# Second mixture's token sums on VectorE, sums and decoding dealt over other steps, an earlier sigmoid table, longer strings of products

## The chip, the cores and the metric

The kernel runs on one core of a Trainium2 chip. The metric is the device time of one launch in microseconds (us). Before the change it is 1125.84 us, the median of 3 runs (1125.04 to 1125.88).

## The reference

Attention with a threshold per row (4 batches, 8 heads, 576 tokens, 64 wide), then two feed-forward blocks ("mixtures") of 2304 tokens, 512 wide, 2048 hidden. The weights come as 64-bit floats.

```python
def _moe_ref(x, w_in, w_out):
    h = x @ w_in
    g = h - np.tanh(h)
    return (g @ w_out).astype(np.float32)

def _moe2_ref(x, w_in, w_out):
    h = x @ w_in
    g = h * (1.0 / (1.0 + np.exp(-h)))
    return (g @ w_out).astype(np.float32)
...
    x = np.ascontiguousarray(attn_out.transpose(0, 2, 1, 3)).reshape(B * S, H * D)
    x = _moe_ref(x=x, **moe_kwargs)
    return _moe2_ref(x=x, **moe2_kwargs)
```

## The kernel before

Every product is made of three TensorE products: each operand is split into a high part, rounded to the TensorE format, and a low part, the rest. A split is a copy on ScalarE and a subtraction on VectorE or GpSimd. A block of weights is decoded from 64-bit words: a DMA into one of three staging slots of `st_r` (`fill`, L749 and L751), a scaling on ScalarE (`rebias`, L757), three integer operations on VectorE (L761, L762, L765), and for `w_out` a high copy on ScalarE (L776) and a low subtraction on GpSimd (L778). `lone` does this for one 128-row block of a `w_out`, `decode_pair` for two blocks of `w2_in` with four GpSimd sums more. Both are generators; `advance` makes one go on to its next yield, and the tables `LONE`, `PAIR`, `EARLY2` and `late` say in which step that happens.

**Attention** takes the first 330 us and is not changed.

**First mixture.** A unit is one 128-wide chunk m of the hidden layer of one tile j of tokens (tiles of 512, 512, 512, 256, 512; 16 chunks: 80 units). Step s of `step_of` writes out, in this order: the 12 products of h for unit s+3 (`emit_h`, L671), the tail of the activation of unit s+1 (`back_a`: L701, L702), the head of that of unit s+2 (`front_a`, ScalarE L683 to L685), `decoding(s, 0)`, `front_b` (GpSimd L690, ScalarE L691 with tanh, VectorE L692), the split of g for unit s+1 (`back_b`: ScalarE L709, VectorE L710), `front_c` (ScalarE L696), pieces of the second mixture (`firsts`, `split_block`), the 12 output products of unit s (`triples`, L722), and `decoding(s, 1)`. The last tile is steps 64 to 79 (`first` = 64).

**Second mixture.** Tokens are taken in three sweeps of 768, the hidden layer in 8 groups g of two chunks, so there are 24 groups. In a group the four quarter products are made from seven (k = 0 to 6), with sums of token quarters (`combos`, recorded at L872 and the high copies at L875) on one side and sums of weights, made by `decode_pair`, on the other. One k is a *slot*. A slot is one string of six 384-wide products (L1024) into one of two banks in turn, then `POPS[k]` output units taken from a queue (`stream`), three 512-wide products each (L978). The bank is read by an addition on VectorE (L1031), for k = 0 by a copy on ScalarE (L1051), for k = 2 by sigmoid and product directly. Four results of a group then go through sigmoid (ScalarE L1054), product (VectorE L1055), high copy (ScalarE L1058) and low subtraction (VectorE L1059), and three output units join the queue. A finished output bank is copied out at L983 (ScalarE) or L985 (VectorE). The sums for the first sweep are `firsts`, made in steps 68 to 76 of the last tile, four entries a step; those for a later sweep are made in the last two groups of the sweep before it. They work in place in the token buffer `xT`, in the pieces of `wr`, and in `st_r`. In `combos`, V is VectorE and G is GpSimd. The 72 loads of weight blocks (`load_block`, L900) each wait for TensorE to have read the buffer; their split is at L905 and L906.

PE, VectorE, ScalarE and GpSimd run their instructions in the order written; SyncE issues all DMAs in its own fixed order.

Of the kernel before, what the change touches and what calls it, by code (L numbers as in the profile page):

```python
# [16 lines left out]
P = 128  # L17
# [23 lines left out]
LONE = ((0, 1), (1, 1), (2, 0), (2, 0), (2, 1), (3, 0))  # L41
PAIR = ((0, 1), (1, 1), (2, 0), (2, 1), (3, 1), (4, 0), (4, 1))
STA = 3
STAGE0 = 10
RATE1 = 15
# [12 lines left out]
def kernel(  # L58
# [86 lines left out]
    if True:  # L145
# [500 lines left out]
        wos = {}  # L646
# [99 lines left out]
        def fill(x, src):  # L746
# [21 lines left out]
        def lone(src, wt):  # L768
# [6 lines left out]
            word = low.bitcast(F32)  # L775
            nc.scalar.copy(out=wt[:, 0], in_=word)  # L776
            yield
            nc.gpsimd.tensor_tensor(out=wt[:, 1], in0=word, in1=wt[:, 0].bitcast(F32), op=ALU.subtract)  # L778
            yield

        def decode_pair(g):
# [10 lines left out]
            low, high = fill(0, source(g))  # L792
# [4 lines left out]
            yield  # L797
            low, high = fill(0, source(g + NG))
# [11 lines left out]
            yield  # L810
# [6 lines left out]
        for m, at in chunks:  # L817
            for ds, pos in LONE:
                due.setdefault((max(-4, at + ds), pos), []).append(m)
        EARLY2 = {0: 65, 1: 68, 2: 71, 8: 74}  # L820
        LATE2 = (9, 10, 3, 11, 4, 12, 5, 13, 6, 14, 7, 15)
        for m, at in EARLY2.items():
            for ds, pos in LONE:
                due.setdefault((at + ds, pos), []).append((1, m))
        for g in range(NG):
            for ds, pos in PAIR:
                due.setdefault((STAGE0 + 4 * g + ds, pos), []).append((2, g))
        running = {}
# [24 lines left out]
        wbuf = [wflat[:, x * (WB + NPC * 2 * HT):][:, 0:WB] for x in range(2)]  # L853
        piece = [wflat[:, WB + i * 2 * HT:WB + (i + 1) * 2 * HT].rearrange("p (c t) -> p c t", c=2) for i in range(NPC)]
# [12 lines left out]
        def combos(s, w2, wx, w1, cs=slice(0, 2)):  # L867
# [9 lines left out]
            V, G = nc.vector, nc.gpsimd  # L877
# [13 lines left out]

        def block(i, b):
# [15 lines left out]
        def step_of(s):  # L908
# [19 lines left out]
            if s == first:  # L928
# [183 lines left out]
```

## Time and profile before

| | |
|---|---|
| median of 3 runs | 1125.84 us |
| profiled execution | 1125.29 us |
| its span, first to last instruction | 1123.5 us |
| PE busy | 1089.6 us (97%) |
| VectorE, ScalarE, GpSimd busy | 857.0 (76%), 784.3 (70%), 433.8 us (39%) |
| first mixture, about | 330 to 727 us |
| second mixture, about | 727 to 1118 us |

In the trace PE is TensorE's products and PEld its weight loads, DVE is VectorE, ACT ScalarE, POOL GpSimd, SP the queue of SyncE. A row of a timeline reads: start, length, engine, line, operation, what it writes and reads, how many were merged, and in brackets the idle time before it with what ended it. A product's length overlaps the next one's; start to start is what counts.

### The profile page before, as it was taken

How to read it: one execution, taken by the hardware profiler on the slowest of the kernel's cores; microseconds unless marked ns; L12 is line 12 of the kernel's file. 1: busy time of each engine (PE TensorE's matmuls, PEld its weight loads, DVE VectorE, ACT ScalarE, POOL GpSimd, SP SyncE). 2: the span in 40 equal slices, each digit the busy share in tenths (PEclk: the TensorE clock that was granted, in tenths of full speed). 3: DMA queues.
4: the chain of work that ended last, by engine and by line, in shares of the span. 5: the costliest groups of instructions: out<-in, count | busy, mean ns of one | idle time of the engine just before them, and what ended most of it. 6: DMA issues, size and time to landing. Idle time of an engine off the chain costs nothing. (4 is left out here: it accounts for less than half of the span.)

```text
span 1123.5 us, 17914 instructions
## 1 busy us (share of the span) xinstructions
PE 1089.6 (97%) x6028; PEld 899.5 (80%) x6028; DVE 857.0 (76%) x1524; ACT 784.3 (70%) x1627; POOL 433.8 (39%) x446
## 2 busy tenths in 40 slices
PE   7999999999999999999999999999999999999998
PEld 6667677767667888888889988789887888879896
DVE  6888888888858878878855677889879655775554
ACT  5988989899878887787877888755544434543432
POOL 4766766777634424434532237612125000110000
PEclk9999999999999999999999999999999999999999
DMA  8677776877534103323311011244423222232211
GB/s 197 155 182 200 202 201 171 220 192 187 160 120 185 56 20 132 131 76 115 133 72 39 11 60 30 64 149 136 132 57 87 80 64 57 61 104 66 57 34 56
DMA packets 104298, 124.93 MB, mean 111 GB/s; under 512 B 47760, under 2 KB 71824, under 8 KB 103184
## 3 DMA queue, kind: packets, MB, share of 16 engines
q1 hardware_dynamic: 104208, 123.80, 38.6%
q8 instruction: 48, 0.79, 0.3%
q14 instruction: 42, 0.34, 0.1%
HBM read 73.93 MB, written 17.30 MB: 81 GB/s over the span
## 5 line engine op out<-in xcount | busy, mean ns | idle before, releaser
L722 PE MATMUL bank<-g_r,wo 128*128 128x512 f32 (+1 forms) x960 | 213.2, 370 | 4.4 <-DVE g_r L710 4.4
L1024 PE MATMUL bank<-wr 128*128 128x384 f32 x816 | 201.1, 336 | 6.2 <-ACT tm_r L1051 3.4
L722 PEld LDWEIGHTS bank<-g_r,wo 128*128 128x128 f32 x960 | 169.3, 190 | 35.5 <-DVE g_r L710 5.5
L671 PE MATMUL bank<-xs_r,wr 128*128 128x512 f32 (+1 forms) x640 | 193.3, 368 | 0.0
L690 POOL TENSOR_TENSOR tm_r<-tm_r 128x512 f32<-128x512 f32 (+1 forms) x78 | 95.7, 1227 | 210.1 <-ACT tm_r L685 210.1
L1024 PEld LDWEIGHTS bank<-wr 128*128 128x128 f32 x816 | 148.4, 188 | 19.5 <-ACT tm_r L1051 4.3
L356 POOL TENSOR_SCALAR e<-e,den 128x576 f32<-128x576 f32 x144 | 119.4, 841 | 55.2 <-DVE den L352 40.3
L671 PEld LDWEIGHTS bank<-xs_r,wr 128*128 128x128 f32 x640 | 117.2, 189 | 20.4 <-ACT st_r L757 0.4
L341 DVE SCALAR_TENSOR_TENSOR e<-s,c,e 128x576 f32<-128x576 f32 x144 | 115.7, 814 | 13.6 <-ACT e L318 13.5
L314 DVE TENSOR_REDUCE c<-s 128x1 f32<-128x576 f32 x144 | 108.4, 754 | 22.7 <-PE s L298 18.8
L671 PE MATMUL bank<-xT,wr 128*128 128x512 f32 (+1 forms) x320 | 117.7, 368 | 0.0
L978 PE MATMUL bank<-wo,xs_r 128*128 128x512 f32 x432 | 116.0, 395 | 0.5 <-DVE xs_r L1059 0.5
L978 PE MATMUL bank<-wo,g_r 128*128 128x512 f32 x432 | 115.0, 393 | 0.0
L318 ACT ACTIVATE e<-s,c 128x576 f32<-128x576 f32 x144 | 106.4, 739 | 0.2
L1054 ACT ACTIVATE tm_r<-tm_r 128x384 f32<-128x384 f32 x72 | 37.8, 526 | 90.2 <-DVE tm_r L1031 90.1
L1031 DVE TENSOR_TENSOR tm_r<-bank,tm_r 128x384 f32<-128x384 f32 x120 | 66.5, 554 | 36.4 <-PE bank L1024 35.9
L692 DVE TENSOR_TENSOR tm_r<-bank,tm_r 128x512 f32<-128x512 f32 (+1 forms) x80 | 50.8, 635 | 53.6 <-ACT tm_r L691 53.4
L361 PE MATMUL t<-ident,e 128*128 128x128 f32 x576 | 83.4, 281 | 8.0 <-POOL e L356 7.6
L978 PEld LDWEIGHTS bank<-wo,g_r 128*128 128x128 f32 x432 | 80.0, 188 | 12.7
L361 PEld LDWEIGHTS t<-ident,e 128*128 128x128 f32 x576 | 61.9, 141 | 34.9 <-POOL e L356 28.6
L978 PEld LDWEIGHTS bank<-wo,xs_r 128*128 128x128 f32 x432 | 79.4, 188 | 11.9 <-DVE xs_r L1059 1.7
L906 DVE TENSOR_TENSOR wr<-wr 128x512 fp32r<-128x512 f32 x96 | 69.0, 719 | 12.7 <-ACT wr L905 12.7
(127 smaller groups left out, 2123.5 us busy)
## 6 DMA issues: line engine op xcount, KB each, us to landing
wr<-pair SPq DMA_DIRECT2D x72, 256.0 KB, 2.9
st_r<-in_moe_w_out_dram SPq DMA_DIRECT2D x24, 512.0 KB, 3.6
kh<-kh SPq DMA_DIRECT2D x60, 144.0 KB, 2.8
raw<-in_moe_w_in_dram SPq DMA_DIRECT2D x16, 512.0 KB, 5.2
st_r<-in_moe_w_in_dram SPq DMA_DIRECT2D x16, 512.0 KB, 3.6
pair<-st_r SPq DMA_DIRECT2D x8, 1024.0 KB, 3.9
qp<-qh SPq DMA_DIRECT2D x30, 160.0 KB, 3.4
qp<-ql SPq DMA_DIRECT2D x30, 160.0 KB, 3.8
```

Source lines behind the costliest of these rows:

```text
L314: nc.vector.tensor_reduce(out=self.c[:, x:x + 1], in_=self.s[x], axis=AX.XY, op=ALU.max, negate=True)
L318: nc.scalar.activation(out=e.rearrange("p (a b) -> p a b", a=2), in_=self.s[x], func=ACTF.Exp, bias=self.c[:, x:x + 1], scale=1.0)
L341: nc.vector.scalar_tensor_tensor(out=e2, in0=self.s[x], scalar=self.c[:, 2 + x:3 + x], in1=e2, op0=ALU.is_ge, op1=ALU.mult, accum_out=self ...
L356: nc.gpsimd.tensor_scalar(out=e, in0=e, scalar1=self.den[:, 2 + x:3 + x], scalar2=1.0, op0=ALU.mult, op1=ALU.mult)
L361: nc.tensor.transpose(t[:, c, :], self.e[x][:, c * P:(c + 1) * P], ident)
L671: nc.tensor.matmul(out=h, lhsT=wi[:, a, cs], rhs=b, start=(c == 0 and x == 0), stop=(c == KD - 1 and x == 2))
L690: (nc.vector if u[0] == 0 and u[1] in PM else nc.gpsimd).tensor_tensor(out=r, in0=r, in1=uu, op=ALU.mult)
L722: nc.tensor.matmul(out=o, lhsT=wo[:, a, cs], rhs=b, start=(m == 0 and x == 0), stop=(m == KF - 1 and x == 2))
L906: nc.vector.tensor_tensor(out=lo, in0=lo.bitcast(F32), in1=hi.bitcast(F32), op=ALU.subtract)
L978: nc.tensor.matmul(out=o, lhsT=l[:, cs], rhs=r, start=(g == 0 and low and x == 0), stop=(g == NG - 1 and not low and x == 2))
L1024: nc.tensor.matmul(out=acc, lhsT=w[:, at(a, c):at(a, c) + P], rhs=b[:, c], start=(k not in (2, 5, 6) and c == 0 and x == 0), stop=(c == 1 ...
L1031: add = lambda out, in0: nc.vector.tensor_tensor(out=out, in0=acc, in1=in0, op=ALU.add)
```

## The change

- In `combos`, V and G are both VectorE: per sweep's set 8 sums that GpSimd made (16 half-wide ones for the first sweep).
- `firsts` begin at step 64 rather than 68 and are dealt by the table `FN`, 36 entries over 12 steps. The first loads of weight blocks move from step 68 to 72, their splits from steps 71 to 74 to steps 73 to 76. The token pieces and the two weight buffers trade places in `wr`.
- The sigmoid table is loaded by a one-element sigmoid directly behind the last ScalarE operation of the last unit of the first mixture.
- `POPS` changes from (1,2,2,1,2,2,2) to (0,1,2,1,3,1,4): the same 12 output units in a group, in longer strings; slot 0 and slot 1 have nothing between them.
- The tables of the decoding move: the eight `w_out` blocks of the first mixture start at steps 2 to 9, one a step (before, the first two in steps -4 and -3, the rest over steps 0 to 7); pairs start two steps later, with the same distance; the early blocks of the second mixture at steps 63, 66, 70, 74 (before 65, 68, 71, 74); in the second mixture the scaling comes one slot earlier, in the same slot as its fill.

```diff
-LONE = ((0, 1), (1, 1), (2, 0), (2, 0), (2, 1), (3, 0))
+LONE = ((0, 1), (0, 1), (1, 0), (1, 1), (2, 1), (3, 0))
...
+FN = (1, 1, 3, 0, 6, 1, 1, 4, 7, 2, 5, 5, 0)
...
         def lone(src, wt):
...
-            yield from words_of(low, high, low, True)
-            yield
             word = low.bitcast(F32)
+            wt = wos[w, m] = wo_p.tile([P, 2, DM], F32R, tag=f"wo{m}", name="wo")
             nc.scalar.copy(out=wt[:, 0], in_=word)
...
-        chunks = [((0, m), m - NW - 4 if m < NW + 2 else (m - NW - 2) * RATE1 // 10) for m in range(NW, KF)]
+        chunks = [((0, m), LONE0 + (m - NW) * RATE1 // 10) for m in range(NW, KF)]
...
-        EARLY2 = {0: 65, 1: 68, 2: 71, 8: 74}
+        EARLY2 = dict(zip((0, 1, 2, 8), SOON))
...
-            V, G = nc.vector, nc.gpsimd
+            V = G = nc.vector
...
-            if s == first + 4:
+            if s == first + F0:
...
+            if s == first + SPLIT0 - 1:
                 for b in range(4):
                     load_block(0, b)
-            for _ in firsts[0:4]:
+            for _ in firsts[0:FN[s - first] if firsts else 0]:
                 firsts.pop(0)()
-            if 0 <= s - first - 7 < 4:
-                split_block(0, s - first - 7)
+            if 0 <= s - first - SPLIT0 < 4:
+                split_block(0, s - first - SPLIT0)
...
-        POPS = (1, 2, 2, 1, 2, 2, 2)
...
-                late.setdefault(3 * i + (0, 3, 3, 4, 5, 6)[x], []).append((1, m))
+                late.setdefault(3 * i + LATEX[x], []).append((1, m))
...
             front_c(units[NU - 1])
+            nc.scalar.activation(out=tm_r[0:1, 8 * HT:8 * HT + 1], in_=c_t[0:1], func=ACTF.Sigmoid)
             for go in triples(units[NU - 3]):
                 go()
```

With `F0` = 0, `SPLIT0` = 9, `LONE0` = 2, `RATE1` = 10, `LATEX` = (2, 3, 2, 4, 5, 6). The rest of the diff asserts that no buffer is used too early.

VectorE's order where the first mixture begins, behind the last split of the tokens. In `bank_4723` and `bank_4724` are h of units 0 and 1. Before, up to the row ahead of the subtraction of g for unit 0 (L710 on `g_r`):

```order
L761 TENSOR_SCALAR st_r<-st_r 128x512
L762 SCALAR_TENSOR_TENSOR st_r<-st_r 128x512
L765 SCALAR_TENSOR_TENSOR st_r<-st_r 128x512
L690 TENSOR_TENSOR tm_r<-tm_r 128x512
L692 TENSOR_TENSOR tm_r<-bank_4723,tm_r 128x512
L701 TENSOR_TENSOR tm_r<-bank_4723,tm_r 128x512
L702 COPY_PREDICATED tm_r<-tm_r 128x512
L761 TENSOR_SCALAR st_r<-st_r 128x512
L762 SCALAR_TENSOR_TENSOR st_r<-st_r 128x512
L765 SCALAR_TENSOR_TENSOR st_r<-st_r 128x512
L690 TENSOR_TENSOR tm_r<-tm_r 128x512
L692 TENSOR_TENSOR tm_r<-bank_4724,tm_r 128x512
```

and now, to that subtraction (L719) and one row beyond:

```order
L699 TENSOR_TENSOR tm_r<-tm_r 128x512
L701 TENSOR_TENSOR tm_r<-bank_4723,tm_r 128x512
L710 TENSOR_TENSOR tm_r<-bank_4723,tm_r 128x512
L711 COPY_PREDICATED tm_r<-tm_r 128x512
L699 TENSOR_TENSOR tm_r<-tm_r 128x512
L701 TENSOR_TENSOR tm_r<-bank_4724,tm_r 128x512
L719 TENSOR_TENSOR g_r<-tm_r,g_r 128x512
L710 TENSOR_TENSOR tm_r<-bank_4724,tm_r 128x512
```

The six decoding operations of two blocks are gone from here; they stand behind the activations of later units.

ScalarE's order where the second mixture begins, from the last activation of unit 79 to the first sigmoid. `bank_4719` is an output bank of unit 79. Before:

```order
L696 ACTIVATE tm_r<-tm_r,cols 128x512
L1051 COPY tm_r<-bank_4723 128x384
L905 CAST wr<-wr 128x512
L709 CAST g_r<-tm_r 128x512
L905 CAST wr<-wr 128x512
L728 COPY tm_r<-bank_4719 128x512
L1054 ACT_TABLE_LOAD
L1054 ACTIVATE tm_r<-bank_4723 128x384
```

and now:

```order
L705 ACTIVATE tm_r<-tm_r,cols 128x512
L1023 ACT_TABLE_LOAD
L1023 ACTIVATE tm_r<-cols 1x1
L1078 COPY tm_r<-bank_4723 128x384
L928 CAST wr<-wr 128x512
L794 CAST wo<-st_r 128x512
L718 CAST g_r<-tm_r 128x512
L928 CAST wr<-wr 128x512
L1081 ACTIVATE tm_r<-bank_4723 128x384
```

The table load moved ahead of the copy for k = 0, the output copy moved behind the first sigmoid, and a decoding copy (L794) came in.

VectorE's order in the last group of a sweep, from the product of k = 4 to the additions of k = 5 and 6. Before:

```order
L1055 TENSOR_TENSOR tm_r<-tm_r 128x384
L872 TENSOR_TENSOR wr<-st_r,wr 128x768
L1031 TENSOR_TENSOR tm_r<-bank_4723,tm_r 128x384
L1059 TENSOR_TENSOR xs_r<-tm_r,xs_r 128x384
L1055 TENSOR_TENSOR tm_r<-tm_r 128x384
L1031 TENSOR_TENSOR tm_r<-bank_4724,tm_r 128x384
```

and now:

```order
L1082 TENSOR_TENSOR tm_r<-tm_r 128x384
L890 TENSOR_TENSOR xT<-st_r,wr 128x2x384
L890 TENSOR_TENSOR wr<-st_r,wr 128x768
L890 TENSOR_TENSOR st_r<-xT,st_r 128x768
L1058 TENSOR_TENSOR tm_r<-bank_4723,tm_r 128x384
L1086 TENSOR_TENSOR xs_r<-tm_r,xs_r 128x384
L1082 TENSOR_TENSOR tm_r<-tm_r 128x384
L890 TENSOR_TENSOR xT<-xT,wr 128x2x384
L1058 TENSOR_TENSOR tm_r<-bank_4724,tm_r 128x384
```

Two sums joined the one behind k = 4, and one came in behind k = 5, all ahead of work that reads a bank.

## Rows read from the trace of the kernel before

**Rows 1.** Waits of PE from 300 us on: us in total, times, longest.

```profile
PE bank L722 <- DVE g_r L710: 4.4, 3, 2.2
PE bank L1024 <- ACT tm_r L1051: 3.4, 2, 1.7
```

**Rows 2.** Timeline, PE: first product of slot 0 of groups 0, 1, 2, 8, 9, 16, 17.

```profile
726.69 0.33 PE L1024 MATMUL bank<-wr 128*128 128x384 f32 x1
...
744.76 0.33 PE L1024 MATMUL bank<-wr 128*128 128x384 f32 x1
...
760.47 0.33 PE L1024 MATMUL bank<-wr 128*128 128x384 f32 x1
...
855.00 0.33 PE L1024 MATMUL bank<-wr 128*128 128x384 f32 x1
...
874.18 0.33 PE L1024 MATMUL bank<-wr 128*128 128x384 f32 x1
...
983.98 0.33 PE L1024 MATMUL bank<-wr 128*128 128x384 f32 x1
...
1002.51 0.33 PE L1024 MATMUL bank<-wr 128*128 128x384 f32 x1
```

**Rows 3.** Timeline, PE: output products of unit 0, and an undisturbed string of twelve.

```profile
344.15 4.37 PE L722 MATMUL bank<-g_r,wo 128*128 128x512 f32 x11 [2.11 <-DVE g_r L710]
...
361.98 2.88 PE L722 MATMUL bank<-g_r,wo 128*128 128x512 f32 x12
```

**Rows 4.** Stages: stretch, length, busy us of PE, PEld, DVE, ACT, POOL, granted clock, DMA.

```profile
345.00:346.00 1.00, 1.00 (x4) 0.81 (x3) 0.55 (x1) 1.00 (x2) 0.26 (x1) 0.50 1.03 418
```

**Rows 5.** Timeline, DVE: last decoding operation before unit 0's subtraction, and that subtraction.

```profile
340.65 0.70 DVE L765 SCALAR_TENSOR_TENSOR st_r<-st_r 128x512 uint32<-128x512 uint32 x1
...
342.46 1.63 DVE L710 TENSOR_TENSOR g_r<-tm_r,g_r 128x512 fp32r<-128x512 f32 x1
```

**Rows 6.** Timeline, end of the last tile: PE, and DVE and POOL before it.

```profile
724.06 2.79 PE L722 MATMUL bank<-g_r,wo 128*128 128x512 f32 x11 [2.17 <-DVE g_r L710]
...
721.21 1.38 DVE L765 SCALAR_TENSOR_TENSOR st_r<-st_r 128x512 uint32<-128x512 uint32 x1
...
720.59 2.87 POOL L872 TENSOR_TENSOR xT<-xT,wr 128x384 fp32r<-128x384 f32 x2
```

**Rows 7.** Timeline, group 0: table load, addition of k = 1, start of slot 4.

```profile
734.14 1.28 ACT L1054 ACT_TABLE_LOAD   x1
...
732.44 0.55 DVE L1031 TENSOR_TENSOR tm_r<-bank,tm_r 128x384 f32<-128x384 f32 x1
...
736.57 0.45 PE L1024 MATMUL bank<-wr 128*128 128x384 f32 x1 [1.33 <-DVE tm_r L1055]
```

**Rows 8.** Timeline, last group of a sweep: DVE with and without POOL, and a quiet group.

```profile
850.62 0.95 DVE L872 TENSOR_TENSOR wr<-st_r,wr 128x768 fp32r<-128x768 f32 x1
...
853.63 2.21 DVE L1055 TENSOR_TENSOR tm_r<-tm_r 128x384 f32<-128x384 f32 x1
...
855.50 4.17 POOL L872 TENSOR_TENSOR xT<-xT,wr 128x768 fp32r<-128x768 f32 x2
...
900.69 0.56 DVE L1055 TENSOR_TENSOR tm_r<-tm_r 128x384 f32<-128x384 f32 x1 [0.65 <-ACT tm_r L1054]
```

**Rows 9.** Stages, columns as in rows 4: a group with sums, a quiet one.

```profile
842.30:858.00 15.70, 15.70 (x79) 14.10 (x79) 14.09 (x17) 9.17 (x16) 8.78 (x5) 1.00 0.23 59
886.00:901.70 15.70, 15.70 (x80) 14.11 (x79) 9.24 (x17) 6.47 (x14) 0.00 (x0) 1.00 0.21 58
```

**Rows 10.** Timeline, PE: strings of 6, 6 and 12 products, each ended by the next.

```profile
844.55 1.55 PE L978 MATMUL bank<-wo,g_r 128*128 128x512 f32 x6
845.94 1.21 PE L1024 MATMUL bank<-wr 128*128 128x384 f32 x6
846.98 0.86 PE L978 MATMUL bank<-wo,g_r 128*128 128x512 f32 x3
...
1110.95 2.92 PE L978 MATMUL bank<-wo,xs_r 128*128 128x512 f32 x12
1113.71 4.24 PE L978 MATMUL bank<-wo,g_r 128*128 128x512 f32 x18
```

**Rows 11.** DMA issues of the page: transfer, count, KB each, us to landing.

```profile
st_r<-in_moe_w_out_dram SPq DMA_DIRECT2D x24, 512.0 KB, 3.6
```

More of the change, by code (lines that the diff above doesn't have):

```diff
@@ L40 @@
 BENG = 'PE Activation'
-LONE = ((0, 1), (1, 1), (2, 0), (2, 0), (2, 1), (3, 0))
-PAIR = ((0, 1), (1, 1), (2, 0), (2, 1), (3, 1), (4, 0), (4, 1))
+LONE = ((0, 1), (0, 1), (1, 0), (1, 1), (2, 1), (3, 0))
+PAIR = ((2, 0), (2, 1), (2, 1), (3, 0), (3, 1), (4, 0), (5, 0))
 STA = 3
 STAGE0 = 10
-RATE1 = 15
+PSTEP = 4
+LONE2 = ((1, 0), (1, 1), (2, 0), (2, 1), (3, 0), (3, 0))
+LATEX = (2, 3, 2, 4, 5, 6)
+SPLIT0 = 9
+POPS = (0, 1, 2, 1, 3, 1, 4)
+SOON = (63, 66, 70, 74)
+F0 = 0
+FN = (1, 1, 3, 0, 6, 1, 1, 4, 7, 2, 5, 5, 0)
+LONE0 = 2
+RATE1 = 10
 DPOS = 0
@@ L716, in triples @@
             wo = wos[0, m]
+            assert (0, m) not in running
+            ended.add(u)
             def go(i):
@@ L744, with fill @@
         QW = 2 * P
-        def fill(x, src):
+        users = {}
+        def fill(x, src, done=()):
+            for y in {x, *done}:
+                assert users.get(y) not in running, "a slot is filled again too early"
+                users[y] = now[0]
             raw = st_r[:, x]
@@ L790, in tt @@
                 nc.gpsimd.tensor_tensor(out=out, in0=in0, in1=in1, op=op)
-            low, high = fill(0, source(g))
+            low, high = fill(0, source(g), (1, 2))
             yield
@@ L826 @@
             for ds, pos in PAIR:
-                due.setdefault((STAGE0 + 4 * g + ds, pos), []).append((2, g))
-        running = {}
+                due.setdefault((STAGE0 + PSTEP * g + ds, pos), []).append((2, g))
+        running, now = {}, [None]
         def advance(what):
@@ L835, in advance @@
                 else:
-                    wt = wos[w, m] = wo_p.tile([P, 2, DM], F32R, tag=f"wo{m}", name="wo")
-                    running[what] = lone((w1_out, w2_out)[w][m * P:(m + 1) * P, :].bitcast(U32), wt)
-            next(running[what], None)
+                    running[what] = lone((w1_out, w2_out)[w][m * P:(m + 1) * P, :].bitcast(U32), w, m)
+            now[0] = what
+            if next(running[what], True):
+                running.pop(what)
         def decoding(s, pos):
@@ L927, in step_of @@
                 front_c(units[s + 2])
-            if s == first:
+            if s == first - 8:
                 stages[0] = 1
-            if s == first + 4:
+            if s == first + F0:
+                assert users.get(1) not in running and users.get(2) not in running
                 ws = [st_f[:, 2 * DM + x * HT:][:, 0:HT].rearrange("p (c t) -> p c t", c=1) for x in range(3)]
@@ L971, in o_unit @@
             wo = wos[1, m]
+            assert (1, m) not in running
             for i in range(3):
@@ L1020 @@
                         blk, hf = ((0, 0), (0, 1), (1, 0), (1, 1), (2, 0), (2, 1), (3, 0))[k]
+                        assert (i, blk) in parted and (i, blk) not in loaded
                         at = lambda x, c: (4 * blk + x * (2 if blk < 3 else 1) + hf) * QW + c * P
```

19 lines of the change are left out of this document (12 added, 7 removed).

## Prediction

> **What bounds the kernel now.** TensorE does, with holes. The profiled execution takes 1125.29 us, 1.8 us more than its span, and 0.55 us less than the median of the runs; I sum against it. The first view to read is PE's waits from 300 us on [rows 1]: VectorE's subtraction of g holds it three times, ScalarE's copy of k = 0 twice. Waits undercount a hole, so I then read start to start. An undisturbed string of twelve 512-wide output products shows as 2.88 us, so eleven are 2.65 [rows 3]. A quiet group of the second mixture goes from 744.76 to 760.47, which is 15.71 us [rows 2]. What is longer than these is what a reordering can win. Attention is not touched, and its holes stay.
>
> The holes are these.
> (A) Entry of the first mixture: eleven products take 4.37 us after 2.11 us of idling [rows 3], and the granted clock there is 0.50, which is 1.2 GHz of 2.4 [rows 4]. Loss 2.11 + 4.37 - 2.65 = 3.83 us.
> (B) End of the last tile: 2.17 idle and a string of 2.79 [rows 6]. Loss 2.17 + 0.14 = 2.3 us.
> (C) Group 0 takes 744.76 - 726.69 = 18.07 us [rows 2]. Loss 2.36 us.
> (D) Borders of the sweeps: groups 8 and 16 take 19.18 and 18.53 us [rows 2]. Loss 3.47 + 2.82 = 6.29 us.
> Together 14.8 us.
>
> **The change, part by part.**
>
> (A) The subtraction of g for unit 0 runs from 342.46 for 1.63 us, and PE goes on at 344.15. Ahead of it on VectorE stand the decoding operations of a block, the last until 341.35 [rows 3, 5]. The change takes the decoding of two blocks out of this place: three VectorE operations just ahead, two ScalarE copies of some 0.55 us each ahead of unit 1's activation, and a GpSimd subtraction that ran beside the VectorE one. Without these the chain is: unit 1's ScalarE chain about 1.1 us earlier, so its two VectorE operations end near 340.2, and unit 0's subtraction at 340.9, since alone it takes about 0.7. PE needs it at 341.9. The idle 2.11 go, and I expect the 1.2 GHz stretch behind it to go too, since PE no longer stops: 3.8 us. Bounds: 2.1 if the clock falls all the same, 3.8 otherwise. What is late next: the eight blocks now come one a step in steps 2 to 12, and with them VectorE has about 5.9 us of work in a step of 5.44 us (2.7 for the activation, 1.9 for the decoding, the rest from GpSimd running beside it). It falls 0.5 us back in each of six steps, some 3 us. In a steady step g is ready more than 6 us before PE asks for it. That covers it at no cost; the price if the cover were gone is those 3 us. The fills stand in SyncE's queue where they stood. The scaling now follows its fill without a step between: a freed slot's fill is issued about 1.4 us after the copy on ScalarE, lands 3.6 later [rows 11], and ScalarE comes to the scaling one step, 5.4 us, after the copy. That just fits. The pairs start two steps later, in a stretch with the same cover.
>
> (B) At the end of the last tile VectorE's decoding operation takes 1.38 us, twice its 0.70 of rows 5, while GpSimd makes sums [rows 5, 6]. Now VectorE makes the 16 half-wide sums itself, at about 0.47 us start to start, 7.5 us over 11 steps, never above five in a step, and GpSimd is quiet except for one operation a step. The worst step is 72: 2.7 for the activation, 5 x 0.47 for sums, 1.7 for a block's decoding and about 0.4 for interference make 7.2 us against 5.44. It is followed by four steps of about 5.1. So the lag at the end is 0.5 to 1.5 us, and the last units leave 4 us of room, as there is no h behind them. Gain 2.3 us; bounds 0 and 2.5.
>
> (C) In group 0 PE waits 1.33 us behind a table load of 1.28 us on ScalarE ahead of the first sigmoid, and the product behind it [rows 7]. The load now stands behind the last activation of unit 79, where ScalarE waits for PE, so it costs nothing there unless ScalarE comes more than about 1 us late; then it delays the copy of k = 0. But the new POPS bring another wait. The addition of k = 1 ends 6.3 us after the group's start (732.44 + 0.55 - 726.69), behind the last unit's activation on VectorE [rows 2, 7]. Slot 3 needs that bank. Before, slot 3 began 6.65 us after the start; with POPS 0, 1, 2 ahead of it, it would begin at 3 x 1.05 + 3 x 0.70 = 5.25 [rows 10]. So 1.1 us of waiting comes here, and up to 0.5 to 1 more, since the block of step 74 now ends in slot 0 and its GpSimd subtraction falls beside the last unit's VectorE operations. I take 1.6. Gain 2.36 - 1.6 = 0.8 us; bounds 0.2 and 2.4.
>
> The Trainium skill prices the table switch higher: in "ScalarE: Activation LUTs", What ACT_TABLE_LOAD costs, a load of about 1.28 us is followed by a drain of about 1.38. The trace does not show the drain: the sigmoid starts right at the end of the load. By the page the copy of k = 0 would come later, and the gain in (C) would be about 0.4 us smaller.
>
> (D) While GpSimd makes its sums, VectorE operations of 0.56 us take up to 2.21 [rows 8]: seven such around the first border, some 8 us, put the products, then the high copies, then the copy of k = 0 behind. The change moves 8 sums a border to VectorE, at 0.95 us each, 0.87 start to start [rows 8]: about 7 us more of its own work in place of about 8 us of slowing. The balance: a quiet group needs 9.24 of 15.7 us [rows 9]. The last group of a sweep gets seven sums, 9.24 + 7 x 0.95 = 15.9; the one before gets three, 12.1; the one behind gets one and four output copies of 0.69, 12.9. So the work fits in the three groups, but fills the middle one. Walking the queue slot by slot with these lengths, the three sums behind k = 4 end 4.7 us behind that slot's products, the addition of k = 5 at 13.3 us of the group and that of k = 6 at 15.9. In the next group the copy of k = 0 ends at 2.4 where slot 2 wants to start at 2.8, and the addition of k = 1 at 5.0 where slot 3 wants 5.25. No wait, with 0.3 us to spare in two places. I leave 0.3 us a border: gain 6.29 - 0.6 = 5.7 us; bounds 2 and 6.3.
>
> Strings. Per group, before: two strings of three and five of six; now three of three, one each of six, nine and twelve. A string of six takes 1.39, one of twelve 2.76, so 0.02 less than two of six [rows 10]. With one joint of 384-wide products less and two of the others, 0.02 to 0.05 us a group, 24 times: 0.5 to 1.2, I take 0.8. Not below nothing: no product is added. New windows in every group: the copy of k = 0 must now be done 1.75 us after its string rather than 3.15. In a quiet group it ends 0.7 us after it. No wait. The late blocks' scaling, a slot earlier, finds its data landed or waits about 1 us on ScalarE, inside that window.
>
> Sum: 3.8 + 2.3 + 0.8 + 5.7 + 0.8 = 13.4 us. 1125.3 - 13.4 = 1111.9 us.
>
> **Rivals.**
>
> (1) VectorE becomes the bound at the borders. The walk leaves 0.3 us; if the sums cost their full 0.95 and each waits 0.3 more for its high copy, 8 x 0.4 = 3 us are missing at either border, and (D) gives about 1 instead of 5.7. For it: 15.9 us of work in 15.7. Against: the group on either side has 3 us free. 1125.3 - 8.7 = 1116.6 us.
> The Trainium skill speaks for it: "Perfetto Trace Analysis", Identifying the Most-Contended Engine, names the engine of highest occupancy as the one to relieve first, and this change loads VectorE and relieves GpSimd. Here the busy VectorE of the border group is itself swollen by GpSimd (14.09 us, of which three sums are VectorE's own [rows 9]), which is why I give the rule no more than this rival's chance.
>
> (2) The entry does not change: unit 0's own activation is late, not the decoding, or the clock falls anyhow and PE's stop only moves. Then (A) gives 0 to 1: 1125.3 - 9.6 - 0.5 = 1115.2 us. Against: in rows 5 the decoding ends 1.1 us before the subtraction could start.
>
> (3) Slower. ScalarE waits in its queue for a DMA. In the second mixture the scaling of the twelve late blocks stands in the slot of its own fill. If the fill goes out only when that slot is reached, ScalarE stands still up to 3.6 us [rows 11], twelve times. About 1.2 us of it has cover (the window of the copy of k = 0, or of the sigmoid of k = 2), the other 2.4 x 12 = 29 us are PE's. 1125.3 - 13.4 + 29 = 1140.9 us. It decides from about 2.3 us of standing still a block, where the loss reaches 13.4. Against: the fills keep their place in SyncE's order among the loads, and a slot is freed a block earlier.
>
> **How the numbers follow.** Forecast 0.75, 1111.9 us. Rival 1: 0.13. Rival 2: 0.06. Rival 3: 0.04. That the change does about nothing, since each gain is eaten by a wait of its own: 0.02. The low end has all holes closed without residue and the strings at 1.2: 14.8 + 1.2 = 16 us, 1109.2 us. The high end takes in rivals 1 and 2: 1116.6 us. Half a microsecond either way lies between the profiled execution and the median, so the range is 1108.7 to 1117.0. Faster by more than 0.2% (2.25 us, about what a measurement of this kernel tells from no change): 0.94; within: 0.02; slower: 0.04.
>
> **What would show it.** Right: no PE wait on L710's successor at the entry, and a clock of 1.00 from 340 to 350; no hole at the end of the last tile; group 0 between 16 and 18 us with a wait at slot 3 on the addition of k = 1; groups 8 and 16 under 16.5 us, with VectorE operations at 0.56 in them; quiet groups at about 15.67. Wrong: quiet groups longer than 15.71, ScalarE waiting for the fills, or PE waits at the borders on VectorE directly.

## The result and the profile after

The changed kernel takes 1111.83 us, the median of 4 runs (1111.26 to 1113.02), against 1125.44 for the kernel before in the same comparison (1124.56 to 1125.88). The ratio is 0.9881, 95% interval 0.9864 to 0.9898: 13.6 us less. The profiled execution takes 1111.26 us with a span of 1109.5. The prediction was 1111.9.

Of the page of the changed kernel, busy time of each engine:

```profile
PE 1085.7 (98%) x6028; PEld 900.5 (81%) x6028; DVE 847.9 (76%) x1556; ACT 782.1 (70%) x1628; POOL 382.4 (34%) x414
```

Of the waits of PE behind attention, five lines in the kernel before (the two longest stand in [rows 1]), one is left, and it is a new one:

```profile
PE bank L1051 <- DVE tm_r L1058: 1.4, 1, 1.4
```

The entry of the first mixture, now. Timelines of DVE (the subtraction of g for unit 0) and PE (the products that need it), then the stage that answers to [rows 4]:

```profile
339.23 0.68 DVE L719 TENSOR_TENSOR g_r<-tm_r,g_r 128x512 fp32r<-128x512 f32 x1
...
340.59 2.88 PE L733 MATMUL bank<-g_r,wo 128*128 128x512 f32 x12
```

```profile
345.00:346.00 1.00, 1.00 (x6) 0.83 (x5) 0.14 (x1) 1.00 (x3) 0.37 (x1) 1.00 0.04 16
```

The subtraction takes 0.68 us instead of 1.63 [rows 5] and is done 0.7 us before PE asks for it. Twelve products take 2.88 us, as an undisturbed string does, and the granted clock is 1.00.

Timeline of PE, first product of slot 0 of groups 0, 1, 2, 8 and 9:

```profile
719.16 0.33 PE L1051 MATMUL bank<-wr 128*128 128x384 f32 x1
...
736.53 0.33 PE L1051 MATMUL bank<-wr 128*128 128x384 f32 x1
...
752.26 0.33 PE L1051 MATMUL bank<-wr 128*128 128x384 f32 x1
...
846.65 0.33 PE L1051 MATMUL bank<-wr 128*128 128x384 f32 x1
...
862.37 0.33 PE L1051 MATMUL bank<-wr 128*128 128x384 f32 x1
```

Group 0 takes 17.37 us instead of 18.07, group 8 15.72 instead of 19.18, and group 1 15.73 instead of 15.71 [rows 2]. Most quiet groups took 15.69 us before, a little less than group 1, and take 15.73 now. So the holes at the borders are gone without residue, and the quiet groups have become longer. Two stages of the kernel before, the last group of a sweep and the first of the next (groups 7 and 8; columns as in rows 4):

```profile
839.31:855.00 15.69, 15.69 (x80) 14.10 (x79) 13.01 (x17) 9.67 (x17) 5.86 (x3) 1.00 0.23 59
855.00:874.18 19.18, 16.50 (x80) 13.87 (x79) 17.45 (x23) 8.15 (x16) 9.84 (x6) 1.00 0.45 130
```

Group 7 now, and two rows of VectorE's timeline in it, the additions of k = 5 and 6:

```profile
830.92:846.65 15.73, 15.73 (x80) 14.15 (x79) 13.71 (x22) 9.92 (x18) 0.00 (x0) 1.00 0.22 58
```

```profile
843.73 0.55 DVE L1058 TENSOR_TENSOR tm_r<-bank,tm_r 128x384 f32<-128x384 f32 x1
...
846.27 0.55 DVE L1058 TENSOR_TENSOR tm_r<-bank,tm_r 128x384 f32<-128x384 f32 x1
```

VectorE makes seven sums in this group instead of two, and is busy 13.71 us instead of 13.01, only 0.7 us more; GpSimd is idle. In group 8 VectorE is busy 13.18 of 15.72 us, where it was 17.45 of 19.18.

All parts, from the starts of PE's products in the profiled execution of each kernel. "Behind attention" is the span less the start of the first product of h, which comes at a different time in each execution (last section). The last column is a median of 4 runs (strings_2220: 5), but a single run for entry_old, late_pool, idle_pool, first_pool, spread_old, table_late and split_later.

| kernel | first mixture | group 0 | groups 1 to 22 | behind attention | time of the runs, us |
|---|---|---|---|---|---|
| before | 396.07 | 18.07 | 351.90 | 792.9 | 1125.44 |
| changed | 389.63 | 17.37 | 346.02 | 780.0 | 1111.83 |
| changed, again | 389.57 | 17.53 | 346.07 | 780.0 | 1112.99 |
| entry_old | 393.65 | 17.83 | 346.00 | 784.6 | 1117.76 |
| late_pool | 389.62 | 17.52 | 353.01 | 787.0 | 1120.14 |
| idle_pool | 389.58 | 17.39 | 358.80 | 792.6 | 1124.08 |
| first_pool | 390.11 | 18.41 | 346.00 | 781.7 | 1113.09 |
| spread_old | 389.57 | 18.25 | 346.08 | 780.8 | 1114.27 |
| table_late | 389.60 | 17.62 | 346.09 | 780.3 | 1114.05 |
| strings_old | 389.58 | 16.91 | 346.08 | 779.4 | 1112.41 |
| strings_2220 | 389.57 | 16.65 | 349.15 | 782.1 | 1114.05 |
| strings_0222 | 389.59 | 17.17 | 348.42 | 781.9 | 1114.44 |
| split_later | 389.61 | 16.29 | 346.78 | 779.7 | 1113.16 |
| best | 389.57 | 16.83 | 344.49 | 777.7 | 1110.22 |

### The profile page after: what moved, and what is told of

It reads as the page before. It is cut to its first block, busy times and chain, and to the rows that moved or that the text cites. A ratio compares the mean times of both kernels' runs of the same rounds, so it can differ in the third digit from the quotient of the medians.

```text
span 1109.5 us, 17900 instructions
## 1 busy us (share of the span) xinstructions
PE 1085.7 (98%) x6028; PEld 900.5 (81%) x6028; DVE 847.9 (76%) x1556; ACT 782.1 (70%) x1628; POOL 382.4 (34%) x414
## 4 chain that ended last, share of the span: by engine, by line
PE 84%; DVE 6%; ACT 5%; issue 2%; POOL 2%; DMA 1%; SPq 0%; POOLq 0%; ACTq 0%; DVEq 0%
PE bank L1003 18%; PE bank L680 16%; PE bank L1051 16%; PE bank L733 16%; PE a L416 6%; PE s L307 6%; PE t L370 4%; DVE c L323 2%; PE t L380 1%; POOL e L365 1%; ACT e L327 1%; DVE e L350 1%; PE t L227 1%; ACT nat L238 1%; ACT wr L142 1%
## 5 line engine op out<-in xcount | busy, mean ns | idle before, releaser
L1051 PE MATMUL bank<-wr 128*128 128x384 f32 x816 | 197.9, 337 | 1.4 <-DVE tm_r L1058 1.4
L699 POOL TENSOR_TENSOR tm_r<-tm_r 128x512 f32<-128x512 f32 (+1 forms) x78 | 100.3, 1286 | 229.1 <-ACT tm_r L694 220.2
L350 DVE SCALAR_TENSOR_TENSOR e<-s,c,e 128x576 f32<-128x576 f32 x144 | 115.6, 813 | 13.5 <-ACT e L327 13.4
L1003 PE MATMUL bank<-wo,xs_r 128*128 128x512 f32 x432 | 111.1, 393 | 0.0
L1058 DVE TENSOR_TENSOR tm_r<-bank,tm_r 128x384 f32<-128x384 f32 x120 | 66.4, 553 | 35.6 <-PE bank L1051 35.6
L929 DVE TENSOR_TENSOR wr<-wr 128x512 fp32r<-128x512 f32 x96 | 62.0, 646 | 27.9 <-ACT wr L928 27.6
```

The source lines that it names most:

```text
L350: nc.vector.scalar_tensor_tensor(out=e2, in0=self.s[x], scalar=self.c[:, 2 + x:3 + x], in1=e2, op0=ALU.is_ge, op1=ALU.mult, accum_out=self ...
L699: (nc.vector if u[0] == 0 and u[1] in PM else nc.gpsimd).tensor_tensor(out=r, in0=r, in1=uu, op=ALU.mult)
L1003: nc.tensor.matmul(out=o, lhsT=l[:, cs], rhs=r, start=(g == 0 and low and x == 0), stop=(g == NG - 1 and not low and x == 2))
L1051: nc.tensor.matmul(out=acc, lhsT=w[:, at(a, c):at(a, c) + P], rhs=b[:, c], start=(k not in (2, 5, 6) and c == 0 and x == 0), stop=(c == 1 ...
```

## Experiments

Each is the changed kernel with one edit, the last with three.

**What is chance.** The changed kernel once more, without an edit.

> The changed kernel itself once more, to tell what is chance between executions. Theory (the executions of one kernel differ in the first 26 us of attention, by up to some 3 us, and hardly behind it): the part from the first product of h on is 780.0 us within 0.3, groups 15.73 and group 0 17.4, the start of that part anywhere from 329.4 to 332.5, the median 1111 to 1113 us. Rival (the differences lie all over the run): the part behind attention differs by over 0.5 us from 780.0.

1112.99 us (1110.98 to 1113.09), ratio to before 0.9894, 0.9877 to 0.9910. The profiled execution begins with h at 329.21 us and has 780.0 us behind it, as the first had to 0.1 us; group 0 differs by 0.16. So the parts behind attention can be compared between profiles at some 0.2 us, but group 0 only at some 0.5 us: in entry_old, whose edit lies 380 us ahead of it, it takes 17.83 us (why, stands under the end of the last tile). The times of the runs can't be compared at less than 1 to 2 us. The verdicts below go by the parts.

**The entry.**

```diff
-LONE = ((0, 1), (0, 1), (1, 0), (1, 1), (2, 1), (3, 0))
+LONE = ((0, 1), (1, 1), (2, 0), (2, 0), (2, 1), (3, 0))
...
-        chunks = [((0, m), LONE0 + (m - NW) * RATE1 // 10) for m in range(NW, KF)]
+        chunks = [((0, m), m - NW - 4 if m < NW + 2 else (m - NW - 2) * 15 // 10) for m in range(NW, KF)]
...
-                due.setdefault((at + ds, pos), []).append(m)
+                due.setdefault((max(-4, at + ds), pos), []).append(m)
```

> The changed kernel with the w_out blocks of the first mixture decoded at their old steps (-4, -3, then 0 to 7); all else as changed (1111.83 us). Theory (decoding ahead of unit 0's subtraction makes the hole, and PE's stop brings the low clock): PE stands still for about 2.1 us ahead of the output products of unit 0, the granted clock behind it is 0.50 for some microseconds, the loss is 3.8 us, the time 1115.6 us. Rival 1 (the clock falls on its own account, not by the stop): idle of 2.1 us but clock 1.00, 1113.9 us. Rival 2 (the hole was closed by another part of the change): no idle, 1111.8 us.

Timelines of DVE and PE, and the stage behind the stop:

```profile
341.34 0.70 DVE L781 SCALAR_TENSOR_TENSOR st_r<-st_r 128x512 uint32<-128x512 uint32 x1
...
343.15 1.67 DVE L719 TENSOR_TENSOR g_r<-tm_r,g_r 128x512 fp32r<-128x512 f32 x1
...
344.88 4.38 PE L733 MATMUL bank<-g_r,wo 128*128 128x512 f32 x11 [2.11 <-DVE g_r L719]
```

```profile
346.00:347.00 1.00, 1.00 (x4) 0.81 (x3) 0.36 (x2) 1.00 (x3) 0.53 (x1) 0.50 1.06 430
```

The hole is back to the hundredth: 2.11 us of idling, a clock of 0.50, the first mixture 4.0 us longer. The theory stands, and the low clock comes with the stop: the kernel before and entry_old have both here, and the other twelve profiles have neither.

**The borders: whose work, or whose company.** First the sums of the later sweeps go back to GpSimd.

```diff
-            V = G = nc.vector
+            V = nc.vector
+            G = nc.gpsimd if s else nc.vector
```

> The changed kernel with the token sums of the second and third sweep on GpSimd as before (eight 768-wide sums a border); those of the first sweep stay on VectorE. Theory (GpSimd's sums make the holes at the borders): groups 8 and 16 take about 19.2 and 18.5 us rather than 15.73, VectorE operations of 0.56 us take up to 2.2 in the last group of a sweep, loss 6.3 us, 1118.1 us. Rival (the longer strings or the moved decoding closed these holes): groups 8 and 16 stay within 0.5 us of 15.73, 1111.8 to 1112.8 us.

Waits of PE from 700 us on, and VectorE in the last group of a sweep:

```profile
PE bank L1052 <- ACT tm_r L1079: 4.1, 3, 2.0
...
PE bank L1052 <- DVE tm_r L1083: 1.1, 1, 1.1
```

```profile
846.71 2.20 DVE L1083 TENSOR_TENSOR tm_r<-tm_r 128x384 f32<-128x384 f32 x1
```

Groups 8 and 16 take 19.47 and 18.10 us, and 7.0 us come back in all. This leaves open whether the sums come late, at some 2 us each, or whether GpSimd at work makes the rest of VectorE late. So the next kernel keeps the sums on VectorE, and GpSimd makes as many that nobody needs, each with a one-element operation ahead of it (all eight sums of a border are wrapped like the one shown):

```diff
+            scrap = wflat[:, 2 * WB + NPC * 2 * HT:][:, 0:4 * HT]
+            def beside(go, out):
+                def both():
+                    go()
+                    nc.gpsimd.tensor_tensor(out=scrap[0:1, 0:1], in0=out[0:1, 0, 0:1].bitcast(F32),
+                                            in1=out[0:1, 0, 0:1].bitcast(F32), op=ALU.subtract)
+                    nc.gpsimd.tensor_tensor(out=scrap[:, 2 * HT:4 * HT], in0=scrap[:, 0:2 * HT].bitcast(F32),
+                                            in1=scrap[:, 0:2 * HT].bitcast(F32), op=ALU.subtract)
+                return both if s else go
...
-                -3: [sub(G, wx, q22, q12)],
+                -3: [beside(sub(G, wx, q22, q12), wx)],
```

> The changed kernel, sums on VectorE, but behind each of the eight sums of a border GpSimd also makes a 768-wide subtraction on scrap memory that nobody reads (with a one-element operation ahead that ties it to its place). Theory A (GpSimd running beside VectorE slows VectorE, and that delay is what PE waits for): VectorE operations of 0.56 us take 1.5 to 2.2 beside it, some 8 us more work on VectorE a border on top of its own sums, holes of 3 to 8 us in groups 7 to 9 and 15 to 17, time 1118 to 1127 us. Theory B (what was late was the sum itself, some 2 us long on GpSimd, and all that follows on it; the slowing is covered): groups stay at 15.73, 1111.8 to 1112.5 us.

Timelines of DVE and of POOL, then the longest entry of PE's waits:

```profile
846.31 0.55 DVE L1068 TENSOR_TENSOR tm_r<-bank,tm_r 128x384 f32<-128x384 f32 x1
846.78 1.36 DVE L1096 TENSOR_TENSOR xs_r<-tm_r,xs_r 128x384 fp32r<-128x384 f32 x1
848.06 0.55 DVE L1092 TENSOR_TENSOR tm_r<-tm_r 128x384 f32<-128x384 f32 x1
848.52 2.21 DVE L890 TENSOR_TENSOR xT<-xT,wr 128x768 fp32r<-128x768 f32 x1
...
845.65 2.07 POOL L903 TENSOR_TENSOR wr<-wr 128x768 fp32r<-128x768 f32 x1
...
848.26 1.67 POOL L903 TENSOR_TENSOR wr<-wr 128x768 fp32r<-128x768 f32 x1
```

```profile
PE bank L1061 <- DVE tm_r L1068: 7.6, 7, 1.4
```

Groups 7, 8, 15 and 16 take 17.95, 19.87, 18.02 and 19.85 us: 12.8 us of holes for 16 useless operations (and 16 of one element). Theory A stands. The useless operations hold nothing by order either: no idle time of VectorE, ScalarE or PE in the second mixture of this run is put down to GpSimd. In the rows GpSimd works from 845.65 to 847.72 and from 848.26 to 849.93. The addition at 846.31, which reads a bank, has its 0.55 us all the same. The subtraction of two buffers behind it takes 1.36 instead of 0.55 and ends 0.4 us behind GpSimd's operation; the sum at 848.52 takes 2.21 instead of 0.95 and ends 0.8 us behind it. Both look as if they had begun when GpSimd was done (last section).

**The end of the last tile: engine or dealing.** In one kernel GpSimd makes the first sweep's sums at the new places, in the other VectorE makes them at the old places.

```diff
-            V = G = nc.vector
+            V = nc.vector
+            G = nc.vector if s else nc.gpsimd
```

> The changed kernel with the 16 sums of the first sweep that GpSimd made before on GpSimd again, but dealt over steps 64 to 75 as changed. Theory (GpSimd beside VectorE makes the hole at the end of the last tile): idle of about 2.2 us ahead of one of the last units' output products, 1114.1 us. Rival (the dealing over more steps closes it, whichever engine makes the sums): no idle there, 1111.8 us within 0.4.

```diff
-F0 = 0
-FN = (1, 1, 3, 0, 6, 1, 1, 4, 7, 2, 5, 5, 0)
+F0 = 4
+FN = (0, 0, 0, 0, 4, 4, 4, 4, 4, 4, 4, 4, 4)
```

> The changed kernel with the sums of the first sweep on VectorE, but at their old places: four a step in steps 68 to 76. Theory (on VectorE they need the dealing over more steps): four steps and more with 2.7 + 1.9 + 1.7 = 6.3 us of work on VectorE against 5.44 of products, a lag of several us, PE waits 2 to 4 us at the end of the last tile or in group 0, 1114 to 1116 us. Rival (that GpSimd no longer runs beside VectorE is enough): no hole at the end of the last tile, the part behind attention within 0.4 us of 780.0.

Waits of PE from 700 to 740 us, of first_pool and then of spread_old:

```profile
PE bank L1052 <- DVE tm_r L1059: 2.2, 1, 2.2
PE bank L733 <- DVE g_r L719: 0.2, 1, 0.2
```

```profile
PE bank L1051 <- DVE tm_r L1058: 2.2, 1, 2.2
```

Both rivals come nearer than the theories: the hole of 2.3 us at the end of the tile stays closed, to 0.5 us in the one and wholly in the other. The rest shows in group 0, where the wait at slot 3 grows from 1.4 to 2.2 us. Rows of ScalarE, first_pool and then spread_old, in which group 0 begins at 719.75 and 721.26:

```profile
720.75 1.28 ACT L1024 ACT_TABLE_LOAD   x1
```

```profile
722.10 1.28 ACT L1023 ACT_TABLE_LOAD   x1
```

ScalarE comes to the early table load 1.00 and 0.84 us after the group's start, and the copy of k = 0 and what hangs on it come as much later. In the changed kernel it comes there 0.03 us ahead of the start. In all seven profiles that have the new strings, the early load and the splits in place, group 0 less this start is 17.40 to 17.45 us: loads at -0.03, 0.09, 0.42, 0.84 and 1.00 us go with 17.37, 17.53, 17.83 (entry_old), 18.25 and 18.41. Either half of the edit does most; both together are worth 0.8 to 1.7 us over one alone. No run has GpSimd at the old places with the rest of the change, so that the two together make the hole is inferred from the kernel before, which differs in more than these.

**The table load.**

```diff
-            nc.scalar.activation(out=tm_r[0:1, 8 * HT:8 * HT + 1], in_=c_t[0:1], func=ACTF.Sigmoid)
```

> The changed kernel without the early one-element sigmoid, so that the table is loaded ahead of the first real sigmoid, in slot 2 of group 0. The prediction's view (the load is on the path of the product of k = 2): a wait of about 1.3 us comes at slot 4 of group 0, group 0 about 18.5 us, 1112.9 us. Rival (with the new strings PE and VectorE wait for the last unit's activation there anyway, and the load lies beside that wait): group 0 stays within 0.3 of 17.4, 1111.8 us.

ScalarE's timeline (the copy of k = 0, the load ahead of the sigmoid):

```profile
722.95 0.48 ACT L1077 COPY tm_r<-bank 128x384 f32<-128x384 f32 x1 [1.25 <-PE bank L1050]
...
727.98 1.28 ACT L1080 ACT_TABLE_LOAD   x1 [0.28 <-DVE g_r L719]
```

The rival is right: group 0 takes 17.62 us, 0.1 to 0.25 more than with the early load. PE's wait is the same 1.4 us for the addition of k = 1. The load begins behind the subtraction for the last unit, for which that addition has to wait too, so it lies beside work that PE waits for anyway. The copy of k = 0 starts 1.34 us after the group's start here and 1.38 with the early load, so the early load has only just room; where it began later, in the runs above, group 0 was as much longer.

**The wait at slot 3.** In the changed kernel it is this chain (timelines of ACT, DVE and PE):

```profile
719.13 1.28 ACT L1023 ACT_TABLE_LOAD   x1
...
720.54 0.45 ACT L1078 COPY tm_r<-bank 128x384 f32<-128x384 f32 x1
720.90 0.62 ACT L928 CAST wr<-wr 128x512 fp32r<-128x512 f32 x1
...
721.55 0.69 DVE L929 TENSOR_TENSOR wr<-wr 128x512 fp32r<-128x512 f32 x1 [2.10 <-ACT wr L928]
722.16 0.68 DVE L710 TENSOR_TENSOR tm_r<-bank,tm_r 128x512 f32<-128x512 f32 x1
...
725.36 0.55 DVE L1058 TENSOR_TENSOR tm_r<-bank,tm_r 128x384 f32<-128x384 f32 x1
...
725.96 1.33 PE L1051 MATMUL bank<-wr 128*128 128x384 f32 x6 [1.39 <-DVE tm_r L1058]
```

VectorE stands idle for 2.10 us ahead of the split of a weight block (L929), whose ScalarE half waits its turn behind the table load and the copy of k = 0, and the last unit's activation (L710) is queued behind that split. So the split goes one slot later in group 0:

```diff
-                        if k < 4:
-                            split_block(i + 1, k)
+                        if 0 <= k - (i == 0) < 4:
+                            split_block(i + 1, k - (i == 0))
```

> The changed kernel, where only the four splits of weight blocks in group 0 of the second mixture stand one slot later (slots 1 to 4 rather than 0 to 3). Theory (the addition of k = 1 is late since VectorE stands 2.1 us at the split of slot 0, whose ScalarE copy waits behind the table load and the copy of k = 0, and the last unit's activation is queued behind it): the activation of unit 79 on VectorE starts some 2.7 us earlier, no wait at slot 3, group 0 about 15.8 rather than 17.37 us, the part of the run behind attention 1.6 us shorter than 780.0. Rival (the activation itself is late, or the splits are missed in group 1): group 0 and 1 together as long as before, 33.1 us.

Timeline of DVE, and two new waits of PE:

```profile
721.65 0.68 DVE L710 TENSOR_TENSOR tm_r<-bank,tm_r 128x512 f32<-128x512 f32 x1
...
736.82 0.97 PE L1003 MATMUL bank<-wo,xs_r 128*128 128x512 f32 x3 [0.22 <-DVE xs_r L1086]
...
740.78 0.44 PE L1051 MATMUL bank<-wr 128*128 128x384 f32 x1 [0.22 <-ACT tm_r L1078]
```

This execution's group 0 begins 2.2 us later than that of the changed kernel, so the activation starts 2.7 us earlier in its group, and the wait at slot 3 is gone: group 0 takes 16.29 us, 1.1 less. But the work put off makes small waits in groups 0, 1 (16.19) and 3 (16.07), and 0.8 us is given back. Theory and rival are each half right; 0.3 us stays.

**Strings.**

```diff
-POPS = (0, 1, 2, 1, 3, 1, 4)
+POPS = (1, 2, 2, 1, 2, 2, 2)
```

> The changed kernel with POPS back at (1,2,2,1,2,2,2). Theory (the new strings cost 1.4 us at slot 3 of group 0 and 0.04 us in each later group, since a string of 384-wide products goes slower behind strings of three, nine and twelve than behind six): wait at slot 3 of group 0 under 0.3 us, group 0 about 16.0 us, quiet groups 15.69, time 2.2 us under that of the changed kernel, 1109.6 us. The prediction's view (longer strings save 0.02 to 0.05 us a group): quiet groups no shorter than 15.73, and only the wait goes, 1110.4 us or more. Rival (the wait only moves): group 0 stays at 17.4, 1111 us.

and with (2,2,2,0,2,2,2) and (0,2,2,2,2,2,2) in its place:

> The changed kernel with POPS (2,2,2,0,2,2,2): six strings of six 512-wide products a group and none of three, nine or twelve, slot 3 of group 0 begins 7.3 us after the group's start. Theory (strings of six are best for what follows, and the addition of k = 1 is done 6.8 us after the start): no wait at slot 3, at most 0.4 us for the last unit's g, group 0 about 16.0, quiet groups 15.64 to 15.66, time 3.0 us under the changed kernel, 1108.8 us. Rival 1 (only the number of strings counts, six as in the changed kernel): quiet groups 15.73, 1110.4 us. Rival 2 (slot 4 straight behind slot 3 waits for the product of k = 2, which reads its bank): PE waits in every group, 1113 us or more.

> The changed kernel with POPS (0,2,2,2,2,2,2): the same six strings of six, with slots 0 and 1 joined as in the change. Slot 3 of group 0 would begin 5.9 us after the start, so 0.9 us of the wait for the addition of k = 1 stay. Theory: group 0 16.6, quiet groups 15.64 to 15.66, 2.4 us under the changed kernel, 1109.4 us. Rival (only the number of strings counts): quiet groups 15.73, 1111 us.

Waits of PE from 740 us on with (2,2,2,0,2,2,2):

```profile
PE bank L1051 <- DVE tm_r L1082: 3.0, 2, 1.7
PE bank L1003 <- DVE xs_r L1086: 0.9, 2, 0.5
```

Quiet groups take 15.69, 15.64 and 15.64 us as expected, against 15.73 with the long strings. The rest missed: group 0 takes 16.91, 16.65 and 17.17 us where 16.0, 16.0 and 16.6 were expected, and the medians lie 2.8 to 5.3 us above the times expected. None of the three has undisturbed borders: groups 7 and 8 take 16.05 and 15.77, 16.36 and 17.69, 15.99 and 18.20 us. What waits there with (2,2,2,0,2,2,2) is an output unit for its g (L1086), and slot 4 for the product that reads its bank (L1082); with (0,2,2,2,2,2,2) it is mostly slots for an addition (L1058). That long strings late in the group help since they put the output units later, and give that chain more time, is argued and not measured by itself. So the new strings cost 0.04 us in each of 22 groups, 0.9 us together, and 0.5 us in group 0, and bring 0.9 us at the two borders; in all the old strings are some 0.5 us better behind attention (779.4 against 780.0), which the times of the runs don't tell apart.

**Together.** The edit of split_later, strings of six, and long strings only where they pay:

```diff
-POPS = (0, 1, 2, 1, 3, 1, 4)
+POPS = (2, 2, 2, 0, 2, 2, 2)
+EDGE = (0, 1, 2, 1, 3, 1, 4)
...
-                        for _ in range(POPS[k]):
+                        for _ in range((EDGE if g == NG - 1 or g == 0 < s else POPS)[k]):
```

> The changed kernel with the splits of group 0 one slot later, POPS (2,2,2,0,2,2,2), and the changed POPS (0,1,2,1,3,1,4) only in the last group of a sweep and the first of the next. Theory (strings of six are quicker, the long strings pay only at the borders, the wait in group 0 comes from the split): group 0 15.8, quiet groups 15.64, borders 15.7 to 15.8, the part behind attention 780.0 - 1.6 - 18 x 0.09 = 776.8 us, the time 1108.6 us. Rival (the borders need the long strings in the groups around as well): holes of 1 to 3 us in groups 6, 9, 14 or 17, time 1110 to 1113 us.

Timeline of PE, starts of groups 2, 3, 7, 8 and 9:

```profile
751.49 0.33 PE L1052 MATMUL bank<-wr 128*128 128x384 f32 x1
...
767.13 0.33 PE L1052 MATMUL bank<-wr 128*128 128x384 f32 x1
...
829.69 0.33 PE L1052 MATMUL bank<-wr 128*128 128x384 f32 x1
...
845.40 0.33 PE L1052 MATMUL bank<-wr 128*128 128x384 f32 x1
...
861.14 0.33 PE L1052 MATMUL bank<-wr 128*128 128x384 f32 x1
```

Quiet groups 15.64, borders 15.71 and 15.74; group 0 takes 16.83 us, not 15.8, for waits like those of split_later. Behind attention it is 2.3 us shorter than the changed kernel. Its runs have a median of 1110.22 us (1108.90 to 1111.80), ratio to before 0.9870, interval 0.9853 to 0.9887. That is below both kernels by the parts; against the changed kernel the spreads of the runs overlap.

## Why the prediction was right, and where it wasn't

The profiled executions differ by 14.0 us, of which 12.9 lie behind attention. The other 1.1 lie in attention, whose code is the same. Some 0.9 of it is a delay of PE at 70 us that the one profile of the kernel before has and none of the other thirteen; that it is chance is likely and not shown. So the mechanisms forecast as 13.4 us gave 12.9. That the time was met to 0.1 us, in the profile to 0.6, is luck: two errors of 0.9 and 1.5 us went against each other, and attention added 1.1.

- **(A)** 3.8 us forecast, 4.0 measured (entry_old), by the step named: decoding ahead of unit 0's subtraction. Counted from the first product of h, that subtraction ends at 10.4 us and PE asks for it at 11.1, forecast 10.3 and 11.3. The eight blocks in steps 2 to 12 cost nothing, as said; there is no PE wait on VectorE there.
- **(B)** 2.3 forecast; the first mixture is 6.4 us shorter, so 2.4 are left for this. The step was right that the hole goes when VectorE makes the sums itself, but it took the dealing for a part of the cure. Either edit closes the hole at the tile's end, and GpSimd's company alone, with the sums at the new places, leaves 0.5 us of it. The rest shows in group 0, with the late table load.
- **(C)** 0.8 forecast, 0.5 to 0.7 measured; the wait at slot 3 was forecast as 1.1 and up to 1 more, and is 1.4. But three steps of it were wrong. The early table load was taken to save 1.33 us and saves 0.1 to 0.25: the new wait covers the load. It was said to cost nothing unless ScalarE comes about 1 us late; the room is some 0.04 us, and in spread_old and first_pool, where it begins 0.84 and 1.00 us after the group's start, group 0 is 0.9 and 1.0 us longer. (No drain shows: the copy of k = 0 starts 0.13 us behind the end of the load.) And the addition is late not for the last unit's own work but for an idle VectorE ahead of a split.
- **(D)** 5.7 forecast, with 0.3 us a border left over; nothing is left. Groups 5, 6, 8 and 16 are 6.6 us shorter. The walk held: the additions of k = 5 and 6 end 13.36 and 15.90 us after the start of group 7 (843.73 + 0.55 and 846.27 + 0.55 less 830.92), forecast 13.3 and 15.9. Where it erred is the reserve put on top of a walk that showed no wait, and the balance of 15.9 us of VectorE's work in this group, which measured 13.71.
- **Strings** 0.5 to 1.2 us gain forecast, "not below nothing", and quiet groups of 15.67 us; measured a loss of 0.04 us in most quiet groups, some 0.7 us in all. Quiet groups above 15.71 were among the prediction's own signs of being wrong, and they came. The step that failed is that only the joints between strings were counted, and a string of six 384-wide products was taken to last as long behind any other. The 512-wide products did save 0.02. But a string of six 384-wide products takes longer behind a string of three, nine or twelve than behind one of six. PE of the changed kernel behind three products, then of the best one behind six, each ended by the start of the next string:

```profile
732.71 1.22 PE L1051 MATMUL bank<-wr 128*128 128x384 f32 x6
733.77 2.92 PE L1003 MATMUL bank<-wo,xs_r 128*128 128x512 f32 x12
```

```profile
721.46 1.21 PE L1052 MATMUL bank<-wr 128*128 128x384 f32 x6
722.50 1.55 PE L734 MATMUL bank<-g_r,wo 128*128 128x512 f32 x6
```

1.06 against 1.04 us. Over all groups the medians are 1.044 us behind six products and 1.062 to 1.066 behind three or nine. A group's seven strings took 7.34 us before (five of 1.044, two of 1.062) and take 7.40 now (one of 1.044, three of 1.062, one of 1.066, and 2.106 for those of slots 0 and 1 together behind twelve), while the 512-wide ones went from 8.34 to 8.33. That is the 0.04. Why the string before matters is open.

The sum by parts: 13.4 + 0.2 (A) + 0.1 (B) - 0.1 (C) + 0.9 (D) - 1.5 (strings) - 0.1 (from group 23 on, 26.9 us instead of 26.8, which is within chance) = 12.9.

Of the rivals, VectorE did not become the bound at the borders: in its last groups of a sweep it is at 13.71 of 15.73 us and PE waits for nothing. (The stretch that the prediction read for this, 14.09 us in [rows 9], begins 3 us after the start of group 7, and two of its sums, not three, are VectorE's.) The Trainium skill ("Perfetto Trace Analysis", Identifying the Most-Contended Engine) has the engine of highest occupancy optimized first. Here that is TensorE, at 97%, and its holes are what the change closed. Taken for the engines that feed TensorE, as the prediction took it, the rule points at VectorE, at 76%, and would have led the wrong way: the engine that had to be cleared was GpSimd, at 39%, and VectorE took its work and became less busy, 847.9 instead of 857.0 us. The entry did change, and the clock with it. ScalarE waited for a fill in the second mixture once, for 0.6 us, and not twelve times (in the repeat twice, 1.0 us together):

```profile
ACT st_r L773 <- DMA st_r<-in_moe_w_out_dram: 0.6, 1, 0.6
```

It did wait in its queue for DMAs of another kind, which rival 3 did not name: behind each sweep an output copy (L1008) stood for 2.4 to 2.7 us until the output ahead had left its buffer, 7.5 us in all (before, one such wait of 2.4). PE waited for nothing there.

## What to carry to other kernels

Before work is moved off an engine that looks full, see how much of its time is its own: an operation that takes four times as long beside another engine is that engine's cost, and an experiment with useless operations there prices it at once. A wait that is removed uncovers the next, and a wait that is added covers others (here the table load), so gains on one stretch are not to be summed but walked in order. A regular loop is worth measuring for each of its string lengths, since its border and its middle may want different ones.

## What the runs showed of the hardware

**GpSimd beside VectorE.** Between buffers, VectorE's operations of 0.55 to 0.95 us took up to 2.2 us while GpSimd worked, and those that read a bank kept their 0.55. The Trainium skill has this in "SBUF — State Buffer", SBUF: two separate sides: the two engines share a pair of ports as a lock that one of them holds for a whole instruction, and on VectorE's side operations with two inputs in SBUF are among those concerned. The rows agree. At the first border of idle_pool eight VectorE operations were stretched, and each ended behind one of GpSimd's: the 384-wide by 0.41 to 0.43 us, the 512-wide by 0.54 or 0.55, the 768-wide by 0.80. That is 0.12 to 0.15 us less than they take alone (0.55, 0.68, 0.95). One that had begun 0.2 us ahead of GpSimd's (848.06) kept its 0.55.

**Two stops, one fall of the clock.** PE's stop of 2.11 us at the entry was followed by some 3 us at 0.50 in the kernel before and in entry_old. The stop of 2.17 us at the end of the last tile [rows 6] was followed by a clock of 1.00, as was the one of 1.39 us in group 0. Stops of like length differ in this, and the runs do not tell why.

**The start is not the same twice.** The first product of h came at 329.2 to 332.4 us in the fourteen profiles, with no change to the code of attention. The first 20 us of two of them, of the changed kernel and then of strings_old (columns as in rows 4):

```profile
0.00:20.00 20.00, 14.11 (x93) 12.05 (x93) 12.14 (x31) 10.37 (x24) 8.24 (x16) 1.00 0.81 217
```

```profile
0.00:20.00 20.00, 14.82 (x84) 13.11 (x84) 9.56 (x27) 8.47 (x20) 6.22 (x14) 0.83 0.79 213
```

Where the granted clock is 1.00 in them (four profiles), h starts at 329.2 to 330.6; at 0.91 (three) at 329.6 to 330.0; at 0.83 (seven) at 331.3 to 332.4. A single time of this kernel can't tell 2 us, then; the parts of a profile behind that point can.
